# Attention and a SoLU expert layer on one core: the same steps in another order on every engine, some on another engine

## The chip, the cores and the metric

The kernel runs on one core of one Trainium2 chip. The metric is the device time of one execution in microseconds (us). A core has five engines that each work off a queue of their own: TensorE (PE in the profile: matmuls; PEld: its weight loads), VectorE (DVE), ScalarE (ACT), GpSimd (POOL) and SyncE (SP), which here issues all data transfers (DMAs). The queues wait for each other by semaphores only, so the order within a queue is fixed by the program, and an instruction that waits holds up all that stands behind it on its engine.

## The reference

The sum of a pooled and a local attention, followed by one expert layer. All is float32 at the inputs except that the expert's weights come as float64.

```python
B, H, S, D = 8, 8, 576, 64; factor = 4; scale = 1 / sqrt(D)
# pooled: q, k, v averaged over 4 positions, plain softmax attention over 144, each row repeated 4 times
out_up = repeat(sm_attn(q_d, k_d, v_d), 4, axis=2)
# local: only positions with |i - j| < 4
scores = where(mask, scale * q @ k.T, -1e9)
out_local = softmax(scores) @ v
x = (out_up + out_local).transpose(0, 2, 1, 3).reshape(4608, 512)
# expert layer
h = x @ w_in                      # 4608 x 1024
solu = h * softmax(h)
ln = (solu - mean(solu)) / sqrt(var(solu) + 1e-6) * g_ln
out = ln @ w_out                  # 4608 x 512
```

## The kernel before, in words

**Tiles.** Attention runs batch by batch (8 of them). In a batch there are four pairs of heads (`pr`) for the pooled attention and five units of two 64-wide windows (`u`) for the local one. The expert layer runs over 36 tiles of 128 tokens; a tile can start when the attention of its tokens is summed in `x`. Matmuls that need float32 accuracy are made of three in a faster type: a number is split in a high part and a low part (`xh`, `xl`; `uh`, `ul`; weights `wi_h`, `wi_l`, `wo_h`, `wo_l`), and high by high, high by low and low by high are summed. That is why an expert tile has 24 matmuls at L861 (into `h`) and 24 at L985 (into `o`), each in two blocks of 12.

**Names.** In what follows a number behind a name is its tile or its batch and pair. `qp_0_1`, `kp_0`: q and k of a pair, transposed by TensorE (batches 0 and 1; L556), copied to `qT`, `kT` (L262 on ScalarE, L264 on VectorE), and summed over 4 positions to `qd_flat` and `kd` (L418). From batch 2 on VectorE transposes (L462, L466). `sd`, `pd`, `pdt`, `po`: scores, probabilities, their transpose and the output of the pooled attention (L787, L802, L822, L843); its maximum is `mxd` (L794), its reciprocal `rsd` (L809). `sc`, `pl`, `plt`, `xp`: the same of the local one (L606 and L694, L624 and L700, L654, L664 and L752); its maxima are L629, L710 and, with its sums, L724, L727, L728. `vw` and `vs` are loads of v for the two (L304 and L298, L315), `warm` is a pair of filler matmuls on zeros (L1042, 24 of these pairs).

**A tile of the expert layer.** `xh` on ScalarE (L1016), `xl` on GpSimd or VectorE (L1019), matmuls into `h` (L861), maximum `nmx` on VectorE (L869), exponent `e` on ScalarE (L873), product with `h` on VectorE (L876), its mean on GpSimd (L881), centering on ScalarE (L899) or VectorE (L901), a store to DRAM and a load back in another layout (`u`, `v`; L909, L941), transposes on VectorE (L962), `uh` on ScalarE (L968), `ul` on GpSimd or VectorE (L971), matmuls into `o` (L985), scaling on ScalarE (L992) and the store. `h` and `o` have one buffer each: the next tile's first matmul into `h` waits until L876 of the tile before has read it.

**The weights.** 16 pieces (`w`, loaded at L354 as float64) are turned to float32 by ScalarE (`Abs`, L363) and VectorE (L365, L369, L374, L378), and split (L409, L411).

**The order.** The whole computation is first written down as a plan of 2039 steps; a step is a few instructions, mostly one. A table of step numbers, `ORDER`, sets the order in which they are issued, and with that the order of every engine's queue. `OTHER` lists the steps that run on the second of two engines.

```python
def engine(usual, instead):
    return instead if now[0] in other else usual
...
for n in ORDER.split():
    now[0] = int(n)
    fn, args = plan[now[0]]
    fn(*args)
```

Of the kernel before, what the change touches and what calls it, by code (L numbers as in the profile page):

```python
# [26 lines left out]
23 16 165 166 2 4 167 168 169 170 171 24 26 27 25 28 29 3 172 33 32 30 31 173 174 197 17 175  # L27
176 177 178 34 35 36 37 181 38 179 182 64 65 66 41 39 180 183 74 56 40 184 185 186 189 75 49
198 199 200 201 187 14 202 188 76 77 78 42 190 191 192 43 44 193 57 48 50 58 45 104 51 67 68 52
213 21 62 53 105 117 69 409 205 401 194 457 46 54 47 55 20 106 107 195 203 70 71 59 410 129 196  # L30
393 22 118 130 119 394 108 109 131 214 79 80 81 110 84 204 85 417 141 142 9 206 207 208 120 86
72 73 209 210 111 215 153 402 0 121 143 411 412 94 216 217 116 112 87 221 218 60 113 132 211
212 413 95 245 10 414 122 88 395 154 133 140 415 416 96 11 97 418 396 397 398 219 134 123 399
403 164 404 222 400 89 90 91 124 128 155 125 144 405 406 419 420 407 513 220 98 223 514 224 246
82 225 226 63 247 83 248 249 99 100 61 92 515 101 516 93 227 228 6 421 237 102 114 145 250 422
408 423 424 126 103 251 115 127 146 434 435 13 156 157 229 135 136 230 137 231 436 232 233 252
493 147 148 293 494 294 238 239 495 446 668 234 235 149 437 240 496 261 447 158 295 458 152 448
497 459 236 159 138 139 253 449 296 241 460 7 438 318 242 439 498 254 499 297 461 160 500 470
471 472 658 161 482 255 256 18 440 462 319 441 298 299 300 257 150 483 473 320 151 301 429 243
433 474 258 259 430 673 503 244 669 463 464 277 260 686 302 303 469 504 304 505 659 660 321 475  # L40
322 442 5 162 343 344 163 484 485 443 8 476 285 262 263 323 324 19 325 307 506 507 523 674 305
444 445 450 486 670 465 466 517 451 524 264 345 286 487 525 265 287 477 425 266 308 452 478 346
288 675 453 309 310 479 663 480 676 267 347 454 306 671 661 467 488 468 664 526 311 15 665 666
368 426 268 314 348 349 508 509 510 455 456 427 269 289 662 290 369 489 490 687 326 688 699 270
481 700 370 491 271 272 431 891 711 291 292 492 312 278 428 350 351 527 273 511 512 279 327 328
280 528 529 530 274 275 352 281 353 282 712 371 283 501 502 332 518 519 520 276 746 747 748 677
432 531 532 284 313 723 724 315 689 690 672 776 329 330 316 667 333 334 335 336 749 337 777 691
521 522 778 735 533 338 372 534 725 692 339 340 373 331 901 374 779 375 726 376 357 358 359 354
896 886 892 341 342 535 756 377 710 693 694 713 902 727 382 897 898 714 736 355 558 715 757 680
360 361 893 758 894 716 12 695 903 536 537 364 362 899 559 363 887 888 682 538 539 750 365 356  # L50
722 904 378 540 728 379 701 702 380 766 767 366 717 696 697 541 542 383 381 684 384 543 583 560
561 729 737 1 738 739 740 698 385 751 562 703 730 752 753 386 389 633 731 732 718 367 768 769
563 584 733 889 934 634 683 564 565 387 566 678 544 545 719 704 935 705 1127 936 685 585 937
780 938 890 586 587 900 588 547 388 390 589 939 940 567 734 706 572 707 1137 608 741 916 917
546 391 918 679 919 742 609 720 721 895 759 760 590 591 592 920 392 681 708 709 548 770 568 549
593 550 610 611 551 612 743 744 745 951 952 908 552 553 754 755 781 972 973 573 574 569 570 554
941 555 974 921 922 923 761 782 783 1142 597 784 942 613 614 975 317 905 635 771 615 762 616
594 785 924 571 976 1128 772 763 764 765 575 556 1138 773 992 598 962 774 914 617 1139 906 595
943 576 577 578 1132 618 619 775 786 636 637 787 944 811 620 812 599 993 932 1140 579 580 638
639 557 640 909 994 1143 963 953 788 789 954 964 965 907 622 1144 1145 966 1129 977 955 956 967  # L60
957 958 600 601 602 603 1133 1134 925 581 641 1153 642 968 596 604 605 790 791 978 1135 792 836
793 926 969 1130 982 979 1192 910 959 621 623 813 624 983 794 915 814 606 984 927 995 945 933
996 625 1193 626 627 647 628 1157 1158 1159 1160 980 928 946 795 929 815 648 796 947 797 649
798 950 1161 837 1141 582 912 629 816 817 818 819 1136 930 931 948 949 861 862 1348 650 630
1175 651 652 1176 1194 960 1371 838 607 985 839 1131 1174 961 1162 1177 913 1163 1164 643 986
911 981 1178 644 645 840 653 1146 631 646 820 987 988 989 1353 1195 970 997 971 841 842 1213
843 654 655 1354 863 1349 1355 1179 998 656 1356 999 800 801 990 1165 1214 1215 991 821 822 823
1203 1204 1233 1234 1216 1217 1205 1358 825 1196 826 1000 1166 1180 1001 802 803 804 805 1052
1053 806 844 864 865 1151 1350 657 1351 866 827 867 1002 1181 1003 807 868 1359 1360 1361 869
808 632 828 799 1149 829 809 830 1004 1182 1005 831 1206 1207 1027 1167 1006 1168 1183 832 1173  # L70
1155 845 846 847 1235 1343 1344 1345 1197 848 1346 1198 1218 1007 1156 1169 1170 870 824 871
1219 1220 872 833 1028 1008 873 849 850 851 852 1208 1009 1171 1172 874 1209 1210 1010 853 1152
1184 1029 1030 1223 1031 854 834 835 1347 1032 1033 1352 1224 1408 1409 1199 1200 855 875 1034
1035 1102 856 1185 1186 857 858 1236 1225 859 1391 1392 1154 1011 876 877 878 1373 1374 1150
1226 1054 1055 1056 1147 810 1191 1201 1227 879 1362 1202 1375 882 1187 1148 1036 1037 1038
1376 880 881 1393 1377 1378 1039 1077 1078 1584 1365 1188 1389 1221 1016 1372 1189 883 1040
1057 1058 1410 1411 884 1059 1012 1412 1394 1395 1079 1080 1041 1190 1017 1018 1013 1585 1589
1237 1367 1060 1222 1396 1061 1062 1014 1015 1379 1228 1599 1380 1081 1019 1020 1021 1357 1419
885 1022 1082 1211 1420 1083 1212 1042 1063 1421 1084 1422 1085 1066 1229 1381 1423 1382 1023
1590 1024 1238 1230 1231 1232 1239 1240 1586 1086 1025 1439 1043 1594 860 1044 1429 1045 1241  # L80
1383 1064 1103 1440 1441 1104 1366 1430 1431 1067 1591 1592 1442 1242 1368 1046 1105 1048 1047
1049 1243 1244 1106 1068 1107 1108 1109 1587 1369 1363 1091 1390 1065 1588 1087 1026 1397 1245
1246 1110 1050 1600 1398 1399 1111 1112 1595 1069 1070 1088 1071 1089 1384 1072 1596 1597 1247
1424 1385 1386 1268 1073 1248 1293 1249 1074 1364 1075 1610 1601 1294 1092 1093 1425 1413 1269
1270 1414 1602 1449 1426 1432 1094 1250 1400 1095 1096 1407 1450 1451 1415 1271 1433 1434 1116
1051 1097 1113 1114 1115 1387 1272 1435 1416 1098 1117 1370 1648 1401 1251 1436 1090 1252 1257
1118 1273 1603 1099 1274 1100 1417 1388 1810 1418 1649 1650 1402 1253 1443 1119 1437 1651 1632
1633 1634 1635 1318 1319 1295 1636 1637 1296 1297 1120 1121 1452 1254 1255 1076 1638 1815 1122
1403 1404 1405 1406 1438 1298 1299 1101 1300 1123 1444 1445 1275 1446 1427 1453 1428 1301 1614
1615 1616 1617 1800 1652 1618 1619 1653 1654 1447 1655 1258 1631 1454 1455 1448 1456 1660 1276  # L90
1661 1639 1640 1259 1260 1261 1256 1320 1124 1321 1457 1593 1598 1690 1262 1263 1828 1322 1125
1302 1662 1458 1277 1278 1279 1680 1681 1280 1801 1323 1816 1324 1802 1817 1325 1459 1460 1264
1281 1265 1266 1663 1664 1691 1692 1303 1307 1308 1630 1282 1283 1304 1284 1285 1286 1287 1288
1461 1805 1682 1509 1462 1463 1305 1306 1464 1811 1641 1642 1289 1829 1126 1326 1309 1818 1327
1812 1328 1290 1465 1484 1310 1466 1467 1620 1683 1485 1291 1311 1312 1486 1313 1510 1643 1606
1621 1487 1813 1814 1665 1806 1670 1671 1608 1656 1611 1803 1672 1329 1330 1468 1332 1488 1622
1473 1314 1657 1315 1489 1490 1623 1331 1491 1267 1666 1667 1469 1333 1334 1492 1335 1336 1474
1658 1659 1673 1807 1674 1470 1316 1644 1645 1609 1471 1472 1493 1624 1494 1495 1337 1808 1511
1512 1339 1830 1338 1684 1513 1514 1831 1515 1865 1866 1867 1340 1804 1516 1604 1848 1534 1535
# [1055 lines left out]
```

## Time and profile before

| | |
|---|---|
| median of 3 runs | 592.88 us (591.15 to 594.04) |
| span of the profiled execution | 592.8 us (the page gives no other time for it) |
| TensorE busy | 568.5 us, 96% |
| VectorE busy | 468.1 us, 79% |
| ScalarE busy | 335.9 us, 57% |
| GpSimd busy | 317.8 us, 54% |
| DMA moved | 99.58 MB, 168 GB/s mean |

The profile is of one execution; times count from the first instruction. Rows of the timeline read: start in us, length in us, engine, line, operation, what is written and read, shapes, count, and in brackets how long the engine was idle before it and who ended that. Rows of groups read: line, engine, operation, names, shapes, count, then total busy us, mean ns of one, and idle us before them with who ended it. Rows of waits read: who waited for whom, total us, times, longest.

### The profile page before, as it was taken

What the parts mean: (1) busy time and instruction counts of PE and PEld (TensorE: products, weight loads), DVE (VectorE), ACT (ScalarE), POOL (GpSimd) and SP (SyncE); (2) the same over time, 40 slices, a digit from 0 to 9 for tenths busy, and PEclk for the clock granted to TensorE, in tenths of its full rate; (3) what the DMA queues carried; (4) which work ended last, traced back from release to release, by engine and by line L of the source; (5) the groups of instructions that cost most, each with busy time, mean ns of one, the idle gap of its engine ahead of it and who ended that gap; (6) DMA issues with size and microseconds to landing.
All of it is one profiled execution on the core that took longest, in us unless ns stands there. A gap on an engine that the chain in (4) does not pass through costs nothing.

```text
span 592.8 us, 15179 instructions
## 1 busy us (share of the span) xinstructions
PE 568.5 (96%) x5832; PEld 439.3 (74%) x5832; DVE 468.1 (79%) x769; ACT 335.9 (57%) x751; POOL 317.8 (54%) x465
## 2 busy tenths in 40 slices
PE   8789799999989999999999999999999999999996
PEld 5567567677767777777777777787787777778885
DVE  6987999999898989887988968978885854654441
ACT  3577677785555655574457455575445645434443
POOL 2475799577765735485366734354532676242211
PEclk9698999999999999999999999999999999999999
DMA  9998779777787688785897858765535454332331
GB/s 272 237 239 168 162 178 201 184 143 210 178 190 179 147 235 183 173 209 169 194 187 186 203 155 156 214 150 177 159 101 159 133 143 139 106 126 90 124 108 53
DMA packets 207112, 99.58 MB, mean 168 GB/s; under 512 B 163136, under 2 KB 193344, under 8 KB 207040
## 3 DMA queue, kind: packets, MB, share of 16 engines
q1 hardware_dynamic: 207040, 98.61, 66.5%
q8 instruction: 46, 0.75, 0.6%
q14 instruction: 26, 0.21, 0.1%
HBM read 65.54 MB, written 27.79 MB: 157 GB/s over the span
## 4 chain that ended last, share of the span: by engine, by line
PE 72%; DVE 10%; SPq 4%; DMA 4%; issue 4%; POOL 3%; ACT 2%; DVEq 0%; POOLq 0%; ACTq 0%
PE h L861 28%; PE o L985 27%; SPq L285 3%; PE sd L787 2%; PE po L843 2%; PE xp L752 2%; PE pdt L822 2%; PE kp L556 2%; PE warm L1042 2%; PE qp L556 1%; PE sc L694 1%; DMA qm<-in_q_dram 1%; DMA u<-e 1%; POOL xl L1019 1%; PE sc L606 1%
## 5 line engine op out<-in xcount | busy, mean ns | idle before, releaser
L861 PE MATMUL h<-wi_h,xh 128*128 128x512 f32 x288 | 116.6, 405 | 0.9 <-DVE e L876 0.7
L985 PE MATMUL o<-wo_h,uh 128*128 128x512 f32 x288 | 116.4, 404 | 0.8 <-ACT uh L968 0.7
L861 PE MATMUL h<-wi_h,xl 128*128 128x512 f32 x288 | 114.3, 397 | 2.6 <-DVE xl L1019 1.4
L985 PE MATMUL o<-wo_l,uh 128*128 128x512 f32 x288 | 113.9, 395 | 0.0
L861 PE MATMUL h<-wi_l,xh 128*128 128x512 f32 x288 | 113.8, 395 | 0.0
L985 PE MATMUL o<-wo_h,ul 128*128 128x512 f32 x288 | 79.0, 395 | 0.0
L869 DVE TENSOR_REDUCE nmx<-h 128x1 f32<-128x1024 f32 x36 | 43.5, 1209 | 36.0 <-PE h L861 36.0
L873 ACT ACTIVATE e<-h,nmx 128x1024 f32<-128x1024 f32 x36 | 40.1, 1113 | 49.8 <-DVE nmx L869 46.0
L861 PEld LDWEIGHTS h<-wi_h,xl 128*128 128x128 f32 x288 | 54.1, 188 | 16.8 <-POOL xl L1019 2.0
L861 PEld LDWEIGHTS h<-wi_h,xh 128*128 128x128 f32 x288 | 54.1, 188 | 16.0 <-DVE e L876 1.9
L985 PEld LDWEIGHTS o<-wo_h,uh 128*128 128x128 f32 x288 | 54.0, 188 | 15.8 <-issue 1.6
L985 PEld LDWEIGHTS o<-wo_h,ul 128*128 128x128 f32 x288 | 54.0, 188 | 13.3 <-DVE ul L971 0.3
L861 PEld LDWEIGHTS h<-wi_l,xh 128*128 128x128 f32 x288 | 54.1, 188 | 12.0
L985 PEld LDWEIGHTS o<-wo_l,uh 128*128 128x128 f32 x288 | 54.1, 188 | 11.9
L971 POOL TENSOR_TENSOR ul<-v,uh 128x512 fp32r<-128x512 f32 x37 | 48.3, 1312 | 24.7 <-ACT uh L968 20.9
L876 DVE SCALAR_TENSOR_TENSOR e<-h,e 128x1024 f32<-128x1024 f32 x36 | 43.7, 1213 | 16.7 <-ACT e L873 16.5
L968 ACT ACTIVATE uh<-v 128x512 fp32r<-128x512 f32 x70 | 42.5, 623 | 21.0 <-DVE v L962 16.9
L962 DVE STREAM_TRANSPOSE v<-v 128x512 f32<-128x512 f32 x70 | 46.6, 688 | 4.8 <-DMA v<-u 4.8
L992 ACT ACTIVATE osb<-o,s 128x512 f32<-128x512 f32 x36 | 24.6, 682 | 43.3 <-PE o L985 18.3
L1019 POOL TENSOR_TENSOR xl<-x,xh 128x512 fp32r<-128x512 f32 (+1 forms) x31 | 37.6, 1219 | 16.5 <-ACT xh L1016 16.0
L881 POOL TENSOR_SCALAR nmu<-su 128x1 f32<-128x1 f32 x36 | 9.8, 273 | 67.0 <-DVE e L876 56.7
L899 ACT ACTIVATE e<-e,nmu 128x1024 f32<-128x1024 f32 x29 | 33.3, 1148 | 19.7 <-POOL nmu L881 19.7
(122 smaller groups left out, 1142.6 us busy)
## 6 DMA issues: line engine op xcount, KB each, us to landing
u<-e SPq DMA_DIRECT2D x35, 512.0 KB
v<-u SPq DMA_DIRECT2D x140, 128.0 KB
vs<-in_v_dram SPq DMA_DIRECT2D x32, 288.0 KB
out_dram<-osb SPq DMA_DIRECT2D x36, 256.0 KB
qm<-in_q_dram SPq DMA_DIRECT2D x96, 72.0 KB
km<-in_k_dram SPq DMA_DIRECT2D x96, 72.0 KB
vw<-in_v_dram SPq DMA_DIRECT2D x80, 64.0 KB
vw<-in_v_dram SPq DMA_DIRECT2D x40, 128.0 KB
```

Source lines behind the costliest of these rows:

```text
L285: nc.sync.dma_start(t[nm][Q * 32:Q * 32 + 32, pr], src[b, 2 * pr + par, :, dh * 32:dh * 32 + 32].rearrange("(k t) d -> t k d", t=32),)
L861: nc.tensor.matmul(hps[:, n, :], src[:, cc, :], wt[:, cc, n * 512:(n + 1) * 512], start=(cc == 0 and src is xh and wt is wi_h), stop=(cc = ...
L869: nc.vector.tensor_reduce(out=nmx, in_=hf, op=ALU.max, axis=AX.X, negate=True)
L873: nc.scalar.activation(e, hf, AF.Exp, bias=nmx, scale=1.0, accum_out=se)
L876: nc.vector.scalar_tensor_tensor(out=e, in0=hf, scalar=1.0, in1=e, op0=ALU.mult, op1=ALU.mult, accum_out=su)
L899: nc.scalar.activation(e, e, AF.Identity, bias=nmu, scale=1.0)
L962: nc.vector.transpose(vg, vg)
L968: nc.scalar.activation(uh, tp, AF.Copy)
L971: (usual if v is None else engine(usual, nc.vector)).tensor_tensor(out=ul, in0=tp, in1=uh.bitcast(F32), op=ALU.subtract)
L985: nc.tensor.matmul(o, src[:, j, :], wt[:, 4 * g + j, :], start=(g == 0 and j == 0 and src is uh and wt is wo_h), stop=(g == 1 and j == 3 a ...
L992: nc.scalar.activation(osb, o, AF.Copy, scale=s)
L1019: engine(nc.gpsimd, nc.vector).tensor_tensor(out=l, in0=src, in1=h.bitcast(F32), op=ALU.subtract)
```

## The change

Two tables are replaced, `ORDER` and `OTHER`; the steps themselves and all other code stay. Of the tables' 217 lines of difference two may stand for all:

```diff
 ORDER = """
-23 16 165 166 2 4 167 168 169 170 171 24 26 27 25 28 29 3 172 33 32 30 31 173 174 197 17 175
...
+32 34 35 173 10 174 175 24 26 27 25 33 14 28 15 176 177 178 165 29 30 31 36 37 18 181 38 189 64
```

By count of instructions, what changes engine: centerings of the expert layer from ScalarE to VectorE (L899 29 to 20, L901 6 to 15); `xl` from GpSimd to VectorE (L1019 on VectorE 9 to 17); `ul` from VectorE to GpSimd (L971 on VectorE 35 to 32); copies from VectorE to ScalarE (L264 37 to 33); one or two each at L365, L411, L486, L489, L631 and L718. The rest keeps its engine and changes place.

TensorE's queue at the program's start, before:

```order
L1042 MATMUL warm_4_139<-filler_101 128x512
L556 MATMUL qp_0_0_152<-ident_82,qm_0_147 64x96 x12
L556 MATMUL kp_0_167<-ident_82,km_0_148 64x96 x12
L1042 LDWEIGHTS filler_101
L1042 MATMUL warm_3_181<-filler_101 128x512
```

(the fourth of four filler pairs that lead the queue, then the first pair's q and k), and now:

```order
L556 MATMUL qp_0_1_131<-ident_82,qm_0_126 64x96 x12
L1042 LDWEIGHTS filler_101
L1042 MATMUL warm_10_147<-filler_101 128x512
L1042 LDWEIGHTS filler_101
L1042 MATMUL warm_10_147<-filler_101 128x512
L556 MATMUL qp_0_0_154<-ident_82,qm_0_126 64x96 x12
```

The second pair's q leads, and one filler pair stands between each two transposes (`qp_0_0`, `kp_0` and `kp_1` follow so).

SP's queue, loads of batch 1 (`qm_1`, `km_1`, `km_1_3` are its q and k) and of v for batch 0's local attention (`vw_0`), before:

```order
L304 DMA vw_1_2_433<-in_v_dram 64x4x64 x4
L541 DMA km_1_427<-in_k_dram 96x2x384
L541 DMA qm_1_426<-in_q_dram 96x2x384
L541 DMA km_1_427<-in_k_dram 96x2x384
L541 DMA qm_1_3_518<-in_q_dram 96x2x384
L541 DMA km_1_427<-in_k_dram 96x2x384
L304 DMA vw_0_1_613<-in_v_dram 64x4x64 x4
L354 DMA stage_132<-in_moe_w_in_dram 128x1024
L315 DMA vs_0_0_4_627<-in_v_dram 72x4x256
L354 DMA w64_10_649<-in_moe_w_out_dram 128x1024
L304 DMA vw_0_3_676<-in_v_dram 64x4x64 x4
L541 DMA km_1_3_696<-in_k_dram 96x2x384
```

and now:

```order
L541 DMA km_1_405<-in_k_dram 96x2x384
L315 DMA vs_0_0_4_578<-in_v_dram 72x4x256
L354 DMA w64_5_595<-in_moe_w_in_dram 128x1024
L541 DMA km_1_405<-in_k_dram 96x2x384
L541 DMA qm_1_404<-in_q_dram 96x2x384
L541 DMA km_1_405<-in_k_dram 96x2x384
L354 DMA stage_145<-in_moe_w_in_dram 128x1024
L354 DMA w64_10_662<-in_moe_w_out_dram 128x1024
L541 DMA qm_1_3_689<-in_q_dram 96x2x384
L541 DMA km_1_3_781<-in_k_dram 96x2x384
L304 DMA vw_0_0_791<-in_v_dram 64x4x64 x4
L304 DMA vw_0_1_810<-in_v_dram 64x4x64 x4
```

Four groups of `vw` loads stood ahead of the last k load of batch 1 (`vw_0_0` some rows higher); all now stand behind it.

VectorE's queue around the product `e_7` (L876 of tile 7), before:

```order
L962 STREAM_TRANSPOSE v_5_2566<-v_5_2566 128x4x128 x2
L724 TENSOR_REDUCE mxl_3_2_2511<-pl_3_2_2421 128x16
L727 TENSOR_SCALAR mxl_3_2_2511<-mxl_3_2_2511 128x16
L728 RECIPROCAL mxl_3_2_2511<-mxl_3_2_2511 128x16
L724 TENSOR_REDUCE mxl_3_0_2665<-pl_3_0_2585 128x16
L727 TENSOR_SCALAR mxl_3_0_2665<-mxl_3_0_2665 128x16
L728 RECIPROCAL mxl_3_0_2665<-mxl_3_0_2665 128x16
L876 SCALAR_TENSOR_TENSOR e_7_2881,su_7_2884<-h_7_2698,e_7_2881 128x1024
```

and now:

```order
L971 TENSOR_TENSOR ul_4_1_2685<-v_4_2464,uh_4_1_2684 128x512
L1019 TENSOR_TENSOR xl_8_2662<-x_1_1420,xh_8_2661 128x512
L876 SCALAR_TENSOR_TENSOR e_7_2792,su_7_2810<-h_7_2695,e_7_2792 128x1024
L264 COPY pdT_2_1_2808<-pdt_2_1_2795 72x6x48
L264 COPY x_2_2233<-xp_2_1_2770 128x4x116
L577 TENSOR_TENSOR x_2_2233<-x_2_2233,po_2_0_2765 128x576
L962 STREAM_TRANSPOSE v_5_2833<-v_5_2833 128x4x128 x2
L724 TENSOR_REDUCE mxl_3_2_2720<-pl_3_2_2409 128x16
```

The transposes of `v_5` and the two sums of batch 3's local attention (L724 with L727 and L728) stood ahead of the product and now stand behind it.

202 rows, old and new, of tables (ORDER, OTHER) are left out of this document.

## The prediction

> **What bounds the kernel now.** I read the page first (busy shares, slices), then engine time by stage, then who ended TensorE's and VectorE's waits, then the timeline around the place where the two change roles.
>
> ```profile
> span 592.8 us, 15179 instructions
> PE 568.5 (96%) x5832; PEld 439.3 (74%) x5832; DVE 468.1 (79%) x769; ACT 335.9 (57%) x751; POOL 317.8 (54%) x465
> PE   8789799999989999999999999999999999999996
> DVE  6987999999898989887988968978885854654441
> ```
>
> TensorE is busy in nearly all of the span, but a busy PE may hide waits, so the stages matter. VectorE is full in the first third and has room after it.
>
> ```profile
> 0.00:65.40 65.40, 53.62 (x873) 38.97 (x873) 53.61 (x96) 40.05 (x98) 34.02 (x40) 0.87 0.93 222
> 65.40:185.10 119.70, 112.97 (x1425) 85.18 (x1421) 114.12 (x194) 79.74 (x182) 87.74 (x105) 1.00 0.80 181
> 185.10:592.80 407.70, 401.90 (x3540) 315.15 (x3540) 300.41 (x481) 216.15 (x471) 196.04 (x321) 1.00 0.59 155
> ```
>
> Columns: stretch, its length, then PE, PEld, DVE, ACT, POOL busy, granted clock, DMA share, GB/s. From 65.4 (first expert matmul) to 185.1 VectorE works 114.1 of 119.7 us: it sets the pace. From 185.1 on TensorE works 401.9 of 407.7 and VectorE only 300: TensorE sets the pace, and loses 5.8 us, of which about 3.9 lie behind its last matmul. The waits of that stretch and of VectorE before it:
>
> ```profile
> PE h L861 <- POOL xl L1019: 1.2, 2, 0.9
> PE o L985 <- ACT uh L968: 0.7, 1, 0.7
> PE h L861 <- DVE e L876: 0.5, 1, 0.5
> ...
> DVE kd L418 <- ACT kT L262: 3.5, 3, 2.0
> DVE rsd L809 <- ACT smd L806: 2.0, 1, 2.0
> DVE e L876 <- ACT e L873: 1.7, 3, 0.8
> DVE mxd L794 <- PE sd L787: 1.6, 2, 1.4
> DVE sml L638 <- ACT pl L635: 0.7, 1, 0.7
> ```
>
> The roles change at tile 8. `h` has one buffer, so `h_8` can't start before VectorE's multiply `e_7` (L876) has read `h_7`:
>
> ```profile
> 140.08 1.21 DVE L876 SCALAR_TENSOR_TENSOR e<-h,e 128x1024 f32<-128x1024 f32 x1
> 142.61 0.49 PE L861 MATMUL h<-wi_h,xh 128*128 128x512 f32 x1
> 183.84 1.16 DVE L876 SCALAR_TENSOR_TENSOR e<-h,e 128x1024 f32<-128x1024 f32 x1
> 185.07 0.50 PE L861 MATMUL h<-wi_h,xh 128*128 128x512 f32 x1 [0.45 <-DVE e L876]
> 197.15 1.22 DVE L876 SCALAR_TENSOR_TENSOR e<-h,e 128x1024 f32<-128x1024 f32 x1
> 199.45 0.39 PE L861 MATMUL h<-wi_h,xh 128*128 128x512 f32 x1
> 208.96 1.23 DVE L876 SCALAR_TENSOR_TENSOR e<-h,e 128x1024 f32<-128x1024 f32 x1 [0.65 <-ACT e L873]
> 213.22 0.50 PE L861 MATMUL h<-wi_h,xh 128*128 128x512 f32 x1
> ```
>
> These are the pairs `e_4`/`h_5`, `e_7`/`h_8`, `e_8`/`h_9`, `e_9`/`h_10`. At `h_8` TensorE waits (0.45); at `h_9` it comes 1.1 us after its release, at `h_10` 3.0. So the end is: VectorE's work up to `e_7`, then TensorE's own 408 us. The sum below goes by this: work ahead of a gate on VectorE, work behind it on TensorE.
>
> **The change, part by part.** *TensorE's own work* is the same: equal instructions, 381 blocks in both orders, 111 borders between expert blocks (L861, L985) and attention blocks in both. Nothing is gained there; the cover is exact.
>
> *Work ahead of the gates on VectorE.* I counted each form ahead of a gate in both orders and took its mean; the larger ones:
>
> ```profile
> L264 DVE COPY x<-xp 128x464 f32<-128x464 f32 x11 | 6.9, 629 | 1.5 <-PE xp L752 1.5
> L724 DVE TENSOR_REDUCE mxl<-pl 128x16 f32<-128x1024 f32 x10 | 11.9, 1188 | 0.0
> L962 DVE STREAM_TRANSPOSE v<-v 128x512 f32<-128x512 f32 x70 | 46.6, 688 | 4.8 <-DMA v<-u 4.8
> L901 DVE TENSOR_SCALAR e<-e,nmu 128x1024 f32<-128x1024 f32 x6 | 5.1, 854 | 0.3 <-POOL nmu L881 0.3
> L745 DVE STREAM_TRANSPOSE plT<-plT 128x1024 f32<-128x1024 f32 x10 | 12.2, 1225 | 3.3 <-DMA plT<-pl 3.3
> ```
>
> - `e_7`: two L724 (2.4) with their small steps L727 and L728 (1.3), two L962 (1.4) and three L264 copies (1.9) now stand behind it; some L418, L365, L971, L1019 (about 2.5 net) have come ahead. Net 4.4 less. `h_8` could start 4.4 earlier.
> - `e_8`: net 0.5 less; with the 1.1 us of slack of `h_9`, at most 1.5 earlier (TensorE's work behind `h_9` is the same blocks).
> - `e_9`: two L901 (1.7, from ScalarE), one L745 (1.2) and one L730 (1.2) come ahead, five copies and others go: net 1.0 more. `h_10` has 3.0 of slack, so 2.0 would be left, but behind it now stand `pdt_3_0`, `sc_4_4` and `plt_3_4`, ahead of it `sd_3_2` and `pdt_3_1`: some 1.2 us more work behind. Left: 0.8.
> - `e_4`: 2.3 more ahead, 1.3 of slack, but `pdt_2_0` and `plt_2_3` now run ahead of `h_5`, some 1 us less behind it, and TensorE waited again at `h_8`, so that a late `h_5` has room: no new bound.
>
> The tightest gate allows 0.8: **term 1 is -0.8 us**, if VectorE idles as much ahead of the gates as before. Of the 4.4, 3.6 are given back within two tiles.
>
> *The start.* Rows of before:
>
> ```profile
> 4.47 0.66 ACT L363 ACTIVATE w<-stage 128x512 f32<-128x512 f32 x1 [2.47 <-DMA stage<-in_moe_w_in_dram]
> 5.16 0.43 DVE L365 TENSOR_SCALAR w<-w 128x512 f32<-128x512 f32 x1 [2.02 <-ACT w L363]
> 2.28 4.23 PE L1042 MATMUL warm<-filler 128*128 128x512 bf16 x8 [2.28 <-POOL filler L222]
> 6.44 2.19 PE L556 MATMUL qp<-ident,qm 96*64 96x96 f32 x24
> 12.26 1.21 PE L556 MATMUL qp<-ident,qm 96*64 96x96 f32 x24
> 17.34 1.50 DVE L369 TENSOR_SCALAR w<-w 128x512 int32<-128x512 int32 x1
> ```
>
> Now a q load leads SP's queue, and on ScalarE the copy of `qp_0_1` stands ahead of the first weight's Abs. With the q data at about 4.0 (less data than the 512 KB that came by 4.47), 2.2 for the transposes and 0.65 for the copy, Abs ends at 7.5 and VectorE's first real step starts there instead of at 5.16: 2.4 late. Its second key reduction then waits for `kp_0`, which stands behind two filler pairs (4.23 for four, 1.1 each) and two more transposes: about 3.1 of waiting, where before there were 2.2. Together +3.3. Against it, before lost 2.0 at 16.3 to 20, where three weight steps took 0.98, 1.50 and 1.10 beside a busy GpSimd and later 0.42, 0.43 and 0.69; that may not come back. Bounds +1.3 and +3.5; I take **+2.5**, nearer to the upper end, since GpSimd has two steps of that weight in the same stretch.
>
> By the Trainium skill, "TensorE: Matmul & The Clock Gate", Part 1: the clock stands at half by default and is released after a busy window of about 3.4 us. The trace agrees that the first transposes run at half (2.19 against 1.21), but the release came only between 8.4 and 12.3, long after 3.4 us of filler. By the page alone the scattered filler pairs would leave the clock at half longer; that is a rival below.
>
> *The loads.* Behind it SP's queue is another: four groups of small `vw` loads stood ahead of the last k load of batch 1, and stand behind it now.
>
> ```profile
> 24.81 2.80 SPq L304 DMA_DIRECT2D vw<-in_v_dram  x4
> ...
> 40.55 2.58 SPq L304 DMA_DIRECT2D vw<-in_v_dram  x4
> 43.23 0.55 SPq L541 DMA_DIRECT2D km<-in_k_dram  x1
> ...
> 49.47 0.75 DVE L418 TENSOR_REDUCE kd<-kT 128x144 f32<-128x576 f32 x1 [2.03 <-ACT kT L262]
> ...
> 54.02 0.61 DVE L794 TENSOR_REDUCE mxd<-sd 128x3 f32<-128x432 f32 x1 [1.44 <-PE sd L787]
> ```
>
> Each group costs SP 2.6 to 2.8 us of issuing. With three to four groups out of the way batch 1's last q and k come some 8 to 10 us earlier (an estimate from these rows), so both waits of VectorE (2.03 and 1.44) can go. Bounds 0 and -3.5; I take **-3.0**. The `vw` loads now come after them; their first user, `xp_0_0`, stands in TensorE's queue behind all of batch 1's transposes, which covers that.
>
> *Engines.* Nine centerings move from ScalarE to VectorE (L899 to L901) and eight `xl` from GpSimd to it, nearly all behind tile 10, where VectorE has over 100 us of room: cost nothing there; cover is TensorE. With `xl_32` on VectorE a part of the late 1.2 us at `xl` goes, `xl_28` stays on GpSimd. A new order could as well add such waits: bounds -1.2 and +1.5; I take **-0.4**.
>
> Sum: -0.8 + 2.5 - 3.0 - 0.4 = -1.7. The page gives the span, 592.8, which is practically the median of the runs (592.88). So **591.1 us**.
>
> **The rivals.**
> *Faster:* VectorE's later waits (2.0, 1.7 and 0.7 above, all between 127 and 165) go too, because other work stands there now. 591.1 - 4.4 gives 586.7. For it: they are chains of a few steps, which an order can fill. Against: it is open what fills them, and nothing in the orders excludes new ones. Chance 0.36.
> *Slower:* the start is lost and not made up: the clock stays at half until the three filler pairs that now stand behind `sd_0_1`, near 20 us. Start +3.5, loads 0, and two more transposes and a score block at half price (1.0, 1.0 and 0.3 more): -0.8 + 3.5 + 0 - 0.4 + 2.3 = +4.6, so 597.4. It decides if VectorE's key reduction of pair 1 starts later than about 16 us. For it: the eight filler matmuls that began at 2.28 no longer lead. Against: TensorE has 185 - 167 = 18 us of idle time ahead of `h_8` (166.6 busy, 53.6 + 113.0 above). Chance 0.22.
> *Nothing moves:* start and loads cancel, the gate is worth under 1 us: the forecast itself, 590 to 596. Chance 0.42.
>
> **How the numbers follow.** A measurement here can tell about 0.5% (3 us) from no change. Low end: all terms at their good ends and the later waits gone, -0.8 + 1.3 - 3.5 - 1.2 - 4.4 = -8.6: 584. High end: -0.8 + 3.5 + 0 + 1.5 + 2.3 = +6.5: 599. I take 584 to 599; the likeliest case alone is 589 to 595. Faster by over 0.5%: 0.36, within: 0.42, slower: 0.22.
>
> **What would show it.** VectorE's first weight step at 7 to 8 us (start); its wait at the reductions near 50 us gone (loads); `h_8` at 181 to 185, `h_9` within 2 us of 199; TensorE's stretch from `h_8` to the end still 407 to 408. I am wrong if VectorE's idle time before `h_8` differs by over 4 us from the 17.4 of before (185.1 less 53.6 and 114.1), or if TensorE waits over 4 us behind it.

## The result, and the profile after

The changed kernel takes 614.84 us (median of 4 runs, 613.0 to 617.0) against 592.62 us (591.15 to 594.04) for the kernel before on the same chip: 1.038 times as long, 95% interval 1.034 to 1.042. The forecast was 591.1, with 584 to 599 as its range.

The page of the changed kernel, the lines that were shown of before:

```profile
span 613.1 us, 15202 instructions
PE 570.7 (93%) x5832; PEld 441.0 (72%) x5832; DVE 476.1 (78%) x778; ACT 327.8 (53%) x746; POOL 311.1 (51%) x461
PE   6768989999999999996999979999999999999996
DVE  5899999999798767978878766988889675573641
```

TensorE is busy 2.2 us longer in all (570.7 against 568.5), and its row now has two notches, a 6 and a 7, where before there were nines. The stages, cut at the first expert matmul and at `h_8` (columns as in the prediction), and the two stretches from `h_8` to TensorE's last matmul, after and before:

```profile
0.00:66.50 66.50, 47.59 (x868) 35.15 (x869) 56.59 (x101) 39.74 (x98) 32.50 (x37) 0.95 0.79 206
66.50:185.20 118.70, 114.41 (x1427) 86.76 (x1425) 110.04 (x182) 79.89 (x177) 86.41 (x106) 1.00 0.81 182
...
185.18:609.18 424.00, 408.69 (x3542) 319.15 (x3540) 309.43 (x497) 207.50 (x470) 192.23 (x318) 0.98 0.59 151
```

```profile
185.10:588.86 403.76, 401.90 (x3540) 315.15 (x3540) 300.41 (x481) 215.46 (x470) 196.04 (x321) 1.00 0.60 156
```

`h_8` starts where it did. All that this execution lost lies behind it: 424.0 instead of 403.8 us, +20.2. Of these TensorE waited 15.3 instead of 1.9 (+13.4), and its matmuls took 408.7 instead of 401.9 (+6.8) at a granted clock of 0.98. Who ended the waits, over the whole execution:

```profile
ACT e L918 <- DMA u<-e: 37.0, 6, 9.9
...
DVE v L962 <- DMA v<-u: 16.7, 7, 4.5
...
PE h L861 <- DVE e L876: 7.8, 4, 4.3
...
DVE kT L462 <- DMA km<-in_k_dram: 6.8, 4, 4.1
...
PE sc L694 <- ACT pdT L262: 4.7, 1, 4.7
```

The first line has no counterpart in before: ScalarE's square (L918) writes over `e`, so it waits until the store of `u` has read it. The first rows of the start and of the gates, in the order of time:

```profile
7.46 0.43 DVE L365 TENSOR_SCALAR w<-w 128x512 f32<-128x512 f32 x1 [4.32 <-ACT w L363]
...
50.58 0.74 DVE L418 TENSOR_REDUCE kd<-kT 128x144 f32<-128x576 f32 x1
...
54.91 0.61 DVE L794 TENSOR_REDUCE mxd<-sd 128x3 f32<-128x432 f32 x1
...
180.64 1.21 DVE L876 SCALAR_TENSOR_TENSOR e<-h,e 128x1024 f32<-128x1024 f32 x1
185.18 0.50 PE L861 MATMUL h<-wi_h,xh 128*128 128x512 f32 x1
198.25 1.19 DVE L876 SCALAR_TENSOR_TENSOR e<-h,e 128x1024 f32<-128x1024 f32 x1
200.41 0.40 PE L861 MATMUL h<-wi_h,xh 128*128 128x512 f32 x1
```

The loss sits in three places. For the first, `h_10` at 215.4, rows of SP (SPq: issuing), ScalarE, VectorE and TensorE:

```profile
202.68 2.23 SPq L285 DMA_DIRECT2D qm<-in_q_dram  x4
204.95 2.12 SPq L285 DMA_DIRECT2D km<-in_k_dram  x4
207.17 0.44 SPq L909 DMA_DIRECT2D u<-e  x1
...
208.91 0.78 DVE L462 STREAM_TRANSPOSE kT<-km 128x576 f32<-128x576 f32 x1 [4.12 <-DMA km<-in_k_dram]
210.29 1.06 ACT L918 ACTIVATE e<-e 128x1024 f32<-128x1024 f32 x1 [7.02 <-DMA u<-e]
211.08 1.19 DVE L869 TENSOR_REDUCE nmx<-h 128x1 f32<-128x1024 f32 x1
212.36 1.11 ACT L873 ACTIVATE e<-h,nmx 128x1024 f32<-128x1024 f32 x1 [0.93 <-DVE nmx L869]
214.06 1.19 DVE L876 SCALAR_TENSOR_TENSOR e<-h,e 128x1024 f32<-128x1024 f32 x1
215.41 0.47 PE L861 MATMUL h<-wi_h,xh 128*128 128x512 f32 x1 [2.34 <-DVE e L876]
```

`u_7` was ready at 191.6 and is stored at 207.2; eight DMAs of `plT`, eight of `q` and `k` and two of `vw_4_3` stand ahead of it, and `vw_4_3` is read only at 311.8. So two things are late at once: the exponent of tile 9 can't start before the square has run, nor before VectorE, held up by `km`, has its maximum. The other two places are `h_14` at 281 (`u_11` ready 256.3) and the scores `sc_6_2` at 368.6 (`u_18` ready 354.6):

```profile
272.50 0.38 SPq L909 DMA_DIRECT2D u<-e  x1
277.21 1.06 ACT L918 ACTIVATE e<-e 128x1024 f32<-128x1024 f32 x1 [9.87 <-DMA u<-e]
278.39 1.11 ACT L873 ACTIVATE e<-h,nmx 128x1024 f32<-128x1024 f32 x1
281.01 0.47 PE L861 MATMUL h<-wi_h,xh 128*128 128x512 f32 x1 [4.25 <-DVE e L876]
...
361.12 1.11 SPq L909 DMA_DIRECT2D u<-e  x1
365.09 1.06 ACT L918 ACTIVATE e<-e 128x1024 f32<-128x1024 f32 x1 [8.38 <-DMA u<-e]
368.63 1.14 PE L694 MATMUL sc<-kT,qT 64*64 64x64 f32 x32 [4.69 <-ACT pdT L262]
```

Against the median length that each kind of TensorE's blocks has in before, the blocks around the three places are 3.9, 6.4 and 7.2 us too long, 17.5 of the 20.2. In before the largest time from a ready `e` to its store was 5.2 us; here it is 16.2 (`u_11`).

### The profile page after: what moved, and what is told of

It reads as the page before. It is cut to its first block, busy times and chain, and to the rows that moved or that the text cites. A ratio compares the mean times of both kernels' runs of the same rounds, so it can differ in the third digit from the quotient of the medians.

```text
span 613.1 us, 15202 instructions
## 1 busy us (share of the span) xinstructions
PE 570.7 (93%) x5832; PEld 441.0 (72%) x5832; DVE 476.1 (78%) x778; ACT 327.8 (53%) x746; POOL 311.1 (51%) x461
## 4 chain that ended last, share of the span: by engine, by line
PE 59%; DVE 14%; SPq 9%; DMA 7%; issue 4%; ACT 4%; POOL 1%; DVEq 0%; POOLq 0%; ACTq 0%
PE h L861 23%; PE o L985 22%; SPq L740 4%; SPq L285 3%; DMA u<-e 2%; PE po L843 2%; DMA vs<-in_v_dram 2%; PE sc L694 2%; PE sd L787 1%; PE qp L556 1%; DVE w L378 1%; PE pdt L822 1%; PE xp L752 1%; DMA km<-in_k_dram 1%; DVE w L374 1%
## 5 line engine op out<-in xcount | busy, mean ns | idle before, releaser
L861 PE MATMUL h<-wi_h,xh 128*128 128x512 f32 x288 | 117.9, 410 | 7.8 <-DVE e L876 7.8
L971 POOL TENSOR_TENSOR ul<-v,uh 128x512 fp32r<-128x512 f32 x40 | 51.7, 1295 | 43.2 <-ACT uh L968 38.1
L962 DVE STREAM_TRANSPOSE v<-v 128x512 f32<-128x512 f32 x70 | 46.8, 690 | 16.7 <-DMA v<-u 16.7
L876 DVE SCALAR_TENSOR_TENSOR e<-h,e 128x1024 f32<-128x1024 f32 x36 | 43.7, 1213 | 19.6 <-ACT e L873 19.5
L918 ACT ACTIVATE e<-e 128x1024 f32<-128x1024 f32 x35 | 36.8, 1050 | 37.0 <-DMA u<-e 37.0
L915 POOL TENSOR_TENSOR va<-r 128x1 f32<-128x1 f32 x36 | 7.2, 202 | 66.9 <-DVE r L912 66.6
```

The lines of the kernel that those rows point to most:

```text
L861: nc.tensor.matmul(hps[:, n, :], src[:, cc, :], wt[:, cc, n * 512:(n + 1) * 512], start=(cc == 0 and src is xh and wt is wi_h), stop=(cc = ...
L876: nc.vector.scalar_tensor_tensor(out=e, in0=hf, scalar=1.0, in1=e, op0=ALU.mult, op1=ALU.mult, accum_out=su)
L918: nc.scalar.activation(e0, e, AF.Square, accum_out=m2)
L962: nc.vector.transpose(vg, vg)
L971: (usual if v is None else engine(usual, nc.vector)).tensor_tensor(out=ul, in0=tp, in1=uh.bitcast(F32), op=ALU.subtract)
```

## The experiments

The theory from these rows: **late transfers**. What TensorE waits for, it says, goes back, through ScalarE or VectorE, to a DMA that SP issued late, because loads that are read much later stand ahead of it. Rivals: SP has too little time for any order; the moved engines (centerings and `xl` on VectorE); the order of the computing engines. Each kernel below differs from its base only in the tables. "Stretch" is TensorE's time from `h_8` to its last matmul in the profiled execution, "wait" its part that TensorE did not work; before has 403.8 and 1.9, the changed kernel 424.0 and 15.3. The ratio is to the kernel before, with its interval.

| kernel | `h_8` at | stretch | wait | L918 for `u` | median us | ratio |
|---|---|---|---|---|---|---|
| stores | 190.9 | 418.4 | 11.1 | 12.3 | 613.46 | 1.031 (1.025 to 1.038) |
| km | 184.9 | 422.2 | 12.0 | 34.7 | 612.95 | 1.029 (1.022 to 1.036) |
| stores_km | 187.7 | 417.6 | 10.9 | 12.6 | 612.03 | 1.032 (1.024 to 1.040) |
| all3 | 185.0 | 418.5 | 10.8 | 14.3 | 609.92 | 1.023 (1.014 to 1.033) |
| other_b | 201.3 | 435.8 | 21.7 | 28.8 | 646.05 | 1.089 (1.081 to 1.097) |
| hyb_ab | 187.9 | 413.5 | 7.2 | 1.1 | 605.11 | 1.019 (1.012 to 1.027) |
| hyb_ba | 183.1 | 427.3 | 17.3 | 31.1 | 616.94 | 1.039 (1.031 to 1.047) |
| late7 | 180.8 | 403.8 | 1.9 | 0 | 592.06 | 0.999 (0.995 to 1.003) |
| late7b | 183.5 | 411.5 | 6.7 | 8.9 | 600.24 | 1.012 (1.008 to 1.016) |
| loads_b | 186.7 | 403.8 | 1.9 | 2.5 | 596.53 | 1.006 (1.003 to 1.009) |
| edf | 185.3 | 419.2 | 11.0 | 17.2 | 609.12 | 1.028 (1.021 to 1.035) |
| edf2 | 186.0 | 416.1 | 10.8 | 15.7 | 608.90 | 1.028 (1.023 to 1.034) |
| edf3 | 189.5 | 419.2 | 13.6 | 24.7 | 614.17 | 1.038 (1.035 to 1.041) |
| edf4 | 187.5 | 419.2 | 11.7 | 21.0 | 609.59 | 1.025 (1.020 to 1.031) |
| edf5 | 186.2 | 411.6 | 7.9 | 20.5 | 604.59 | 1.020 (1.014 to 1.027) |

`h_8` moves by several us from execution to execution of one and the same start, so effects of 3 to 7 us are read in the stretch, not in the total. The stretch is that of one execution each; before, late7 and loads_b, whose stretches hold no long wait, agree within 0.1 us. In hyb_ba's file the square stands one line later, at L919.

**The three places, one by one (stores, km, stores_km, all3).** SP's queue, here for `u_7`; `u_11`, `u_17` and `u_18` likewise:

```diff
+L909 u_7
 L298 vw_4_3 x2
 L740 plT_3_2 x8
 L285 q and k of batch 4, pair 0, x8
-L909 u_7
```

> The changed kernel, but the stores of u_7, u_11, u_17 and u_18 (L909) stand 3 to 25 instructions earlier in SP's queue: u_7 ahead of the loads of vw_4_3, two groups of plT and the q and k of batch 4's first pair; u_11 ahead of vw_4_0 and two more groups; u_17 ahead of the first half of plT_5_2, u_18 ahead of the loads of v_17. Nothing else moves. Theory 'late stores': ScalarE's square L918 waits for the store, the next exponent stands behind it, then e (L876), then h. The waits of L918 for u near 210, 277 and 365 us (7.0, 9.9, 8.4) shrink to under 2 each; at h_14 6.4 us come back (the excess of the two blocks there), at o_16 7.1; at h_10 nothing, since VectorE still waits 4.1 there for km: 614.8 - 13.5 = 601 us, range 598 to 605. Rival 'SP is short of time': another load is late in place of each store, and the time stays at 612 to 617. Rival 'engine moves' (VectorE is overloaded by the centerings and xl it was given): L918's waits go, but TensorE's three waits stay: 612 to 616.

Measured: at the third place all came back (`h_19` to `h_20` 15.4 us instead of 22.7), at the first nothing, as expected (`h_9` to `h_10` 15.07, was 15.0). At the second the square no longer waits, but the exponent behind it does, now for VectorE, which waits for `plT_4_0`:

```profile
272.11 1.05 ACT L918 ACTIVATE e<-e 128x1024 f32<-128x1024 f32 x1
...
279.44 1.25 DVE L745 STREAM_TRANSPOSE plT<-plT 128x1024 f32<-128x1024 f32 x1 [2.33 <-DMA plT<-pl]
280.61 1.19 DVE L869 TENSOR_REDUCE nmx<-h 128x1 f32<-128x1024 f32 x1
281.89 1.11 ACT L873 ACTIVATE e<-h,nmx 128x1024 f32<-128x1024 f32 x1 [8.65 <-DVE nmx L869]
```

The stretch fell by 5.6 us, not by 13.5. The total hardly moved, since this execution had also started 5.7 us later.

```diff
-L740 plT_3_2 x8
 L285 q and k of batch 4, pair 0, x8
+L740 plT_3_2 x8
```

> The changed kernel, but the eight loads of batch 4's first q and k (L285) stand ahead of the eight DMAs of plT_3_2 (L740) in SP's queue, 5 us earlier; the stores stay late. Theory 'late stores': VectorE's wait for km near 209 us (4.1) goes, but the exponent behind L918 can't start before 211.5 (now 212.4), since u_7 is still stored at 207; h_10 gains 0.8 at most: 613 to 615. Rival 'late loads' (what VectorE waits for is the whole cause at h_10): h_10's wait of 2.3 us and the half clock behind it go, -3.9: 611.

The total is 613, as the theory had it, but the place was disturbed by another wait ahead of it (`h_8` to `h_9` 19.3 us), so this run alone decides nothing.

> Both moves together. Theory 'late stores', with two causes side by side at h_10: all three stalls go, -3.9 -6.4 -7.1 = -17.4: 597.4 us, range 595 to 601; 3.9 less than with the stores alone. Rival 'SP is short of time': the plT groups now come late and VectorE waits for them at L745: 605 or more. Rival 'engine moves': 610 or more.

The total missed: 612.0, where 597.4 was expected. From `h_8` to `h_11` it took 43.8 us; 47.3 in the changed kernel, 46.5 with the stores alone, 47.3 with km alone. So both moves together bring 3.5 us here, which fits two causes side by side at `h_10`; it isn't shown, since km was disturbed ahead of the place, and all3, which has both moves too, took 46.6 us: there TensorE waited 1.8 at `sc_4_0`, behind a late `v`. Then came the second place, with the loads of `vw_5_3` and `vw_4_2` behind `plT_4_0`:

```diff
-L298 vw_5_3 x2
...
-L298 vw_4_2 x2
 L285 q and k of batch 5, pair 0, x8
 L740 plT_4_0 x8
+L298 vw_5_3 x2
+L298 vw_4_2 x2
```

> Stores and km moved as in stores_km, and besides the loads of vw_5_3 and vw_4_2 (not needed before 285 us) stand behind the two plT_4_0 groups in SP's queue, so that batch 5's first q and k and plT_4_0 come 2.7 us or more earlier. In stores_km VectorE waited 2.45 for that km and 2.36 for that plT just ahead of nmx_13, and TensorE then 3.35 at h_14. Theory 'late stores and loads': the wait at h_14 falls below 1 us and its excess (5.4 with the block ahead of it) to about 1: TensorE's blocks from h_8 on are some 7 us over their medians instead of 11.1 (17.5 in the changed kernel). Time by that: 612.0 - 4.4 = 608, and the same start as the changed kernel's profile would make it 604; range 601 to 610. Rival 'SP is short of time': a new wait of over 2 us appears within 40 us behind: 611 to 614.

The total, 609.9, lies at the upper end of the range. `h_13` to `h_14` took 13.05 us (changed kernel 16.7, before 13.7): that stall is gone. The stretch stayed at 418.5, because 3.1 us were lost at `h_17` (VectorE behind a late `km`) and 3.6 at `pdt_3_0` (behind a late `v`). So the stalls at the second and third place went with the late transfers that were named, but then others came through. Here the rival "SP is short of time" was still alive.

**The engines (other_b).** The order of the changed kernel with `OTHER` of the kernel before.

> The changed kernel's order of steps with the kernel before's choice of engines (OTHER alone goes back: 9 centerings and 8 xl leave VectorE again, and so on). Theory 'late stores': the stores stay late, since SP's order is the changed one, and the time stays at 611 to 619. Rival 'engine moves': most of the 22 us come back: 593 to 600.

646 us: not a gain but 31 us more than the changed kernel. In the profiled executions it is 28, 16 of them ahead of `h_8` and 12 behind. So the moves between engines, taken as a whole, did not cost the 22 us; with this order they save time. Single moves weren't tried.

**Where in the program (hyb_ab, hyb_ba).** The table up to `h_8` of one kernel, and the remaining steps in the order and on the engines of the other.

> The changed kernel's steps, in its order and on its engines, up to where its table has h_8; all the other steps in the order and on the engines of the kernel before. Theory 'all of the loss is behind h_8': 593, range 589 to 598, and TensorE's stretch from h_8 on is 406 to 412. Rival 'the first stretch counts too' (a start that varies with DMA and clock, as in the runs of the changed kernel from 609 to 619): 598 to 604, with h_8 at 188 or later.

> The reverse: the kernel before up to where its table has h_8, all the other steps in the changed kernel's order and on its engines. Theory 'all of the loss is behind h_8': 613, range 608 to 617, with waits at the squares L918 of over 5 us as in the changed kernel. Rival 'the first stretch counts too': 600 to 606.

hyb_ba lost all of it, as the theory had it: 427.3 behind `h_8`, with 31.1 us of waiting for `u` at the square. hyb_ab lost 9.4 us at the seam (`h_8` to `h_9` 23.8 instead of 14.4); from `h_9` on it needed 389.8 us, before 389.4. So the loss of the changed kernel behind `h_8` belongs to the order there. The rest of hyb_ab's 12 us is its start: `h_8` at 187.9. Its total, 605.1, missed the theory's range, which had not reckoned with the seam, and is nearer to the rival's: the start counts too.

**One late store in the kernel before (late7, late7b).** The first try did not do what its text says: the steps of one tile run in a fixed order among themselves, and the store could not pass the reciprocal that follows it. It came behind 13 DMAs only, and the steps behind it moved too: ScalarE's square of tile 7, ahead of the exponent of tile 8 in the kernel before, came behind it.

> The kernel before with one step moved: the store of u_7 (L909) stands behind two groups of plT, the q and k of a pair and three more loads in SP's queue, directly ahead of the loads of v_7; it is issued near 200 us instead of 186.5, as late as in the changed kernel. Theory 'late stores': ScalarE's square of tile 7 (194.9) waits to about 203.5, the exponent behind it (195.9) and e_8 go 8 to 9 us later, h_9 starts near 207 instead of 199.5; with a slower clock behind the wait, +8 to +11: 601 to 604. Rival (the store's place has no effect, since v_7 comes at the same time as before): 590 to 596, h_9 at 199 to 200.

The store was issued 6.6 us after its data instead of at once. SP, which before had stood waiting for `e_7` at its queue's head for 2.4 us, ran ahead by about as much; the rest of the 4 us in the text below is that this execution was 4.3 us ahead as a whole. ScalarE came to the square only at 196.7, 7.9 us behind the store's issue, and didn't wait; the time stayed at 592.06. So this run says nothing of a late store with the square in its old place. In the second all queues but SP's stay, except that the reciprocal (two places on VectorE) and a small multiply (one on GpSimd) move with the store:

```diff
-L909 u_7
 L315 vs_3_0
 L740 plT_3_2 x4
 L285 q and k of batch 4, pair 1, x8
 L740 plT_3_2 x4
 L298 vw_3_2 x2
+L909 u_7
```

> The kernel before with the store of u_7 behind two groups of plT, a pair's q and k, and the loads of vw_3_2 (in late7 it had in fact come only behind 13 DMAs, since a tile's steps run in their own order, and SP, no longer waiting for e_7, ran ahead by 4 us). Now 19 DMAs stand ahead of it: issued near 196.5, landed near 200, 5 us after ScalarE reaches the square of tile 7 (194.9, times of the kernel before). Theory 'late stores': exponent and e_8 go 5 us later, h_8 to h_9 takes 18 to 20 us instead of 14.4: 596 to 599. Rival (late stores cost nothing on their own): h_8 to h_9 stays under 15.5, 591 to 594.

First the store's row in before, then the rows of late7b:

```profile
186.51 0.34 SPq L909 DMA_DIRECT2D u<-e  x1
```

```profile
195.66 0.57 SPq L909 DMA_DIRECT2D u<-e  x1
199.24 1.06 ACT L918 ACTIVATE e<-e 128x1024 f32<-128x1024 f32 x1 [5.87 <-DMA u<-e]
200.29 1.10 ACT L873 ACTIVATE e<-h,nmx 128x1024 f32<-128x1024 f32 x1
202.89 0.77 PE L861 MATMUL h<-wi_h,xh 128*128 128x512 f32 x1 [4.83 <-DVE e L876]
```

`h_8` to `h_9` takes 19.4 us instead of 14.4, and the matmuls behind the wait run slower (0.77 for the first): the stretch is 7.7 us longer, 4.8 of waiting and 2.9 of slow clock. The whole kernel is 1.2% slower. One store, issued 9 us later, makes a stall like the three of the changed kernel. That a late store alone, with ScalarE's and TensorE's queues unchanged, does this is shown.

**The loads at the start (loads_b).** The kernel before with this alone:

```diff
-L304 vw_0_0, vw_1_2, vw_0_1, vw_0_3 (x4 each, among the loads of batch 1)
 L541 last k of batch 1
+L304 vw_0_0, vw_1_2, vw_0_1, vw_0_3
```

> The kernel before with one change at the start: the loads of vw_0_0, vw_1_2, vw_0_1 and vw_0_3 (16 DMAs) stand behind the last k load of batch 1 in SP's queue instead of among batch 1's loads, as the changed kernel has it in substance. The prediction's third term: VectorE's waits near 50 and 54 us (2.03 and 1.44) go and h_8 starts 3 us earlier (0 to 3.5): 590, range 588 to 593. Rival: the time comes back as other waits of VectorE before e_7, since its work is a chain through TensorE and ScalarE: within 1 us of the kernel before.

It is slower by 0.6%. VectorE's wait at its sum near 50 us shrinks (0.92 instead of 2.03) and `h_0` comes at 63.6, but other waits stand in their place: a weight piece, and the first `km` of a later batch.

```profile
46.99 0.75 DVE L418 TENSOR_REDUCE kd<-kT 128x144 f32<-128x576 f32 x1 [0.92 <-ACT kT L262]
61.88 0.43 DVE L365 TENSOR_SCALAR w<-w 128x512 f32<-128x512 f32 x1 [1.64 <-ACT w L363]
103.99 0.78 DVE L462 STREAM_TRANSPOSE kT<-km 128x576 f32<-128x576 f32 x1 [1.54 <-DMA km<-in_k_dram]
```

**SP's queue in another order, all else as changed (edf to edf5).** For every transfer behind 180 us I took from the changed kernel's trace when its first reader wanted it, and let the nearest want come first. ScalarE's and TensorE's queues stay word for word; five reciprocals of 0.1 us on VectorE and three small multiplies on GpSimd move by a few places with the stores they follow.

```diff
 L285 q and k of batch 4, pair 3, x8
-L298 vw_4_3 x2
-L740 plT_3_2 x8
 L285 q and k of batch 4, pair 0, x8
 L909 u_7
+L740 plT_3_2 x8
 L941 v_7 x4
...
+L298 vw_4_3 x2
```

> The changed kernel with SP's queue alone put in another order from 180 us on: each transfer has the time at which its first reader wanted it in the changed kernel's profile, less 6 to 9 us, and the nearest comes first; stores, loads back and plT no earlier than their data are there. So the loads of vw that are read 30 to 128 us later step back behind stores, q and k, and plT; no instruction of another engine moves. Worked out with the issue times of the profile (0.45 to 0.65 us each) nothing is late by over 1 us before 300 us. Theory 'SP's order': waits of ScalarE and VectorE for DMAs behind h_8 fall from 38.7 and 29.7 us to under 15 together, and TensorE's stretch from h_8 to its end from 424.0 to 405 to 411; time 596 to 604, by the start. Rival 'SP is short of time' (as the three moves of all3 gave: 424.0 to 418.5, with new waits): 416 or more, 608 or more. Rival 'the order of the computing engines': likewise 415 or more, but with few waits for DMAs left.

VectorE's waits for `km` are gone and those of the squares halved, but the waits for DMAs sum to 50.6 us (under 15 was expected) and the stretch stays at 419.2: `plT_4_0` came 7.5 us late, behind loads that nothing needed yet and behind a load back that stood waiting for its own store.

> A second round of the same: SP's queue alone is put in another order, from 165 us on, now by the times of the edf run, and stores, plT and the loads back go 6 us further ahead of plain loads. In edf plT_4_0 still came 7.5 us late at VectorE (277 us), since loads that are read 30 to 122 us later and a load back that waited for its own store stood ahead of it. Theory 'SP's order': that wait goes, the waits of VectorE and ScalarE for DMAs behind h_8 fall from 50.6 (edf) to under 30, and TensorE's stretch from h_8 to its end from 419.2 to 408 to 414. Rival 'the order of the computing engines': the waits for DMAs fall, but others (for PE, ScalarE, VectorE) take their place: 416 or more. Rival 'SP is short of time': the waits for DMAs stay above 45: 416 or more.

416.1: `h_14` is as early as in before, and one wait of 4.5 us at `o_14` is left, with 6.1 us of excess around it. It leads through VectorE to `v_15`, issued behind the eight loads of a pair that is read 25 us later. VectorE's and ScalarE's waits for DMAs, 37.7 together, had fallen less than said, and the stretch had missed its range by 2 us.

> edf2 with three steps of SP's queue moved: the store of u_15 ahead of batch 6's second pair of q and k, and the third pair of q and k (read 25 us later) behind the store of u_16, so that the load back v_15 is issued near 318 instead of 324.5. In edf2 the one large wait of TensorE left was 4.53 us at o_14 (osb by ScalarE, behind exponents of pd that waited for VectorE, which waited for v_15). Theory 'SP's order': that wait and the block's excess around it (4.6 + 1.5) go: TensorE's stretch from h_8 to its end 409 to 412 (edf2 416.1, the changed kernel 424.0, the kernel before 403.8); time 602 to 606. Rival 'the order of the computing engines': another wait of over 3 us stands in its place, 415 or more.

`h_17` to `h_18` takes 11.3 us, as in before: gone. But the wait at `sc_6_2` was back with 6.75 us. The chain of waits of edf3 has the two stores ahead of it:

```profile
350.65 4.82 DMA u<-e
...
357.84 8.90 DMA u<-e
```

The store of `u_18` was issued earlier than in the changed kernel, but took 8.9 us to land, beside three loads of 288 KB each that are read 50 to 118 us later.

> edf3 with two more changes of SP's queue: the loads vsl_6_3, vsl_6_1 and vsl_6_0 (288 KB each, read 50 to 118 us later) stand behind the store of u_19 instead of around the store of u_18; vw_3_0 and vsl_3_2 stand ahead of batch 5's q and k. In edf3 the wait of edf2 at o_14 was gone, but the store of u_18, issued at 357.8 behind these loads, landed 8.9 us later (in the changed kernel 4.0), and TensorE waited 6.75 at sc_6_2. Theory 'what stands ahead of an urgent transfer, in SP's queue and in the DMA engines': the store lands within 5 us, the wait falls under 1 us, and TensorE's stretch from h_8 to its end is 409 to 412 (edf3 419.2, the changed kernel 424.0, the kernel before 403.8). Rival 'the order of the computing engines needs this wait': a wait of over 3 us stays there or in the next 40 us, 415 or more.

With these loads behind it the store landed in 3.7 us and the wait at `sc_6_2` was gone. Now `plT_4_0` was late again, by 6.4 us, as SP came to it 5 us later than in edf2.

> edf4 with three loads (vsl_4_0, vsl_4_3, vw_5_3, read 26, 62 and 119 us later) behind the store of u_12, and vw_4_1 behind plT_4_0, so that plT_4_0 is issued 3 us earlier. In edf4 the waits of edf2 (o_14) and edf3 (sc_6_2) were both gone, but TensorE waited 1.7, 3.35 and 2.2 between 276 and 291, since plT_4_0 came to VectorE 6.4 us late. Theory 'what stands ahead of an urgent transfer': these waits fall under 1 us together and TensorE's stretch from h_8 to its end is 409 to 413 (edf4 419.2). Rival 'the order of the computing engines', or transfers whose time differs from execution to execution: another wait of over 3 us, 415 or more.

Inside the forecast of the stretch: 411.6, no wait of TensorE over 1.6 us; those between 273 and 289 still sum to 2.6, where under 1 was expected.

```profile
186.23:597.82 411.59, 403.70 (x3542) 315.50 (x3540) 305.56 (x495) 206.88 (x469) 195.15 (x318) 1.00 0.61 155
```

By SP's queue alone, with the computing engines as changed, 12.4 of the 20.2 us came back, 7.4 of waiting and 5.0 of clock. So SP had the time for an order that gives back most of the loss, and "short of time" fell with this run. The four rounds ahead of it had all missed their forecast of the stretch, by 2 to 8 us: each time another transfer was late. The remaining 7.8 stay open: small waits, some behind `v` (VectorE still waits 23.3 us for it in all), some in the order of the computing engines. ScalarE's own order (the square of tile 18 ahead of that of tile 17) wasn't tried. No kernel beat the one before.

## Why the prediction was wrong

- **TensorE's work** is the same, as said: 401.9 us before, 403.7 in edf5. The conclusion drawn from it, that TensorE's stretch from `h_8` to the end takes "still 407 to 408" ("the cover is exact"), is the step that failed: it took 427.9. A bound engine's stretch is its work plus its waits, and I had followed inputs only to `h_10`. For the other 390 us there was one term, the new waits under *Engines*, -0.4 with bounds of -1.2 and +1.5. It measured +20.2: 13.4 of waiting, most of it at three places behind transfers that SP issued late (11.3 us there), and 6.8 of lower clock.
- In particular, of SP's queue I weighed only the start. Behind `h_8` I looked at who ended waits in before, where no square waits for a store; what could newly be late was not gone through, though both orders of SP's queue were there to compare.
- **Engines**: the moves were costed at nothing; other_b shows that this order without them is 31 us slower. The sum was not hurt, but "cover is TensorE" was no measure of it.
- **Start** (+2.5): VectorE's first weight step at 7.46, within the 7 to 8 that I gave.
- **Loads** (-3.0): the two waits near 50 us went, and yet loads_b shows no gain from the move, but a loss of 0.6%. In that run the term has the other sign: the waits were read as a price, but when they went, other waits took their place.
- **Gate** (-0.8): `e_7` came 3.2 us earlier (180.64), but `h_8` did not wait for it; it started at 185.18 without a wait, since TensorE was itself busy 114.4 of the 118.7 us ahead. The sum ahead of `h_8` was -1.3. In this profile it is +0.1; over eleven profiles with the changed start `h_8` comes at 186.9 on average, over four with the start of before at 183.1. So the start cost nearer to +3.8, about what loads_b loses with its one move (3.0 in the median); that the two are the same isn't shown. Before's profile was the latest of its four, and the sum took its span for the time, which in the runs that have both is 1.7 us or more above the span.
- **The slower rival** (0.22) had the sign but not the cause: the granted clock of the first stage is 0.95, before 0.87. VectorE's first two key reductions started at 11.4 and 14.0, not behind 16, so what was to decide for it did not come. The clock fell behind `h_8`, at the three stalls.
- Of my two signs of being wrong, the wait of TensorE behind `h_8` (over 4 us) came: 15.3. VectorE's idle time ahead of `h_8` did not move by 4: 18.6, before 17.4.

## What to carry to other kernels

Where one queue issues all transfers, treat it as an engine: for each transfer set when its reader wants it against when it is issued, and look for loads read 30 to 120 us later that stand ahead of stores on which a buffer's next writer depends. When an engine is busy 96% of its time, equal work says nothing about an order; go through every input of it, to the end of the program, in the new queues. And read a repair at its place in the trace: a total hides that the next late transfer has taken over.

## What the hardware showed

A wait of 2.3 us on TensorE could be enough to halve its rate. The matmuls behind `h_10`'s wait start 0.23 us apart at first, then 0.43, and the granted clock is 0.50 from 216.7 to 220.1:

```profile
215.96 0.40 PE L861 MATMUL h<-wi_h,xl 128*128 128x512 f32 x1
216.19 0.40 PE L861 MATMUL h<-wi_h,xh 128*128 128x512 f32 x1
...
217.47 0.63 PE L861 MATMUL h<-wi_l,xh 128*128 128x512 f32 x1
217.89 0.63 PE L861 MATMUL h<-wi_h,xl 128*128 128x512 f32 x1
```

The Trainium skill, "TensorE: Matmul & The Clock Gate", Part 1, has the clock go back to half after at least one idle window of about 3.4 us. The half rate here lasts about that long, but the idle time ahead of it was 2.3: less than a whole window was enough.

The length of a wait alone doesn't decide. In edf `o_14` waited 2.36 us, as long as `h_10` here, and the matmuls behind it start 0.23 us apart:

```profile
338.96 0.50 PE L985 MATMUL o<-wo_h,uh 128*128 128x512 f32 x1 [2.36 <-ACT osb L992]
339.30 0.40 PE L985 MATMUL o<-wo_l,uh 128*128 128x512 f32 x1
339.54 0.39 PE L985 MATMUL o<-wo_h,uh 128*128 128x512 f32 x1
```

What fits both is where the wait lies. Within one execution the granted clock changes only at points that are multiples of 3.41 us apart: in the changed kernel at 216.72, 220.13, 281.57, 284.98, 366.90 and 373.73. In the piece of 3.41 us that ends at 216.72 TensorE was idle for 2.1 us; in edf such a point cuts the wait in 1.1 and 1.2. Over all profiles, behind `h_8` and with the clock full until then, each of the 23 pieces with more than 1.85 us of idle time was followed by half the clock, and none with less than 1.7. So a stall's price varies with its place: in the changed kernel +6.8 us of clock on +13.4 of waiting, in late7b 2.9 on 4.8.

From its issue to its landing a store of `u` took 3.1 to 4.8 us in the places above, and 8.9 beside three large loads. And issuing is no small thing here: most DMAs hold SP for 0.33 to 0.68 us, and the 668 of them sum to 376 us of the 613 in the changed kernel, 378 of 593 in before.
